# Seven PSUM banks from one pool, two queues of matmuls in product steps, and a block sum copied by VectorE, in a two-attention kernel on one core

## Chip, core and metric

The kernel runs on one core of a Trainium2 chip. The metric is the device time of one execution in microseconds. Before the change it is 1604.68 us, the median of three runs (1604.38 to 1604.77). Engine names are short: PE is TensorE's matmuls and PEld its weight loads, DVE is VectorE, ACT ScalarE, POOL GpSimd, SP SyncE.

## What is computed

Two attentions over 2048 positions, width 576, 32 heads of 18, all in float32. Their outputs stand beside each other in the result.

```python
# A: each position sees 8 positions, 2 apart (W=8, dil=2)
logits = einsum("bhsd,bhswd->bhsw", q, kg) * scale
o = einsum("bhsw,bhswd->bhsd", softmax(where(mask, logits, -1e9)), vg)
a = o.transpose(0, 2, 1, 3).reshape(B, S, D) @ wo
# B: full attention
p = softmax(einsum("bhqd,bhkd->bhqk", q, k) * scale)
o = einsum("bhqk,bhkd->bhqd", p, v)
b = o.transpose(0, 2, 1, 3).reshape(B, S, D) @ wo
return concatenate([a, b], axis=-1)
```

## The kernel before

The work has three stages. In the first (to about 430 us of the span) the inputs are multiplied by the weights; matmuls are written as sums of products of split float32 parts. `stream` deals them to the two halves of the array: rows 0 to 63 and rows 64 to 127 of TensorE each run a matmul of their own at the same time, and "half" below always means that (r = 0 is the lower, r = 1 the upper). Some of B's **maxima** are already made there; `EARLY_PAIRS` (L41) sets how many.

A maximum (`maximum`, `block`, L165 to L241) is a 128x512 block of queries by keys on TensorE (L175) and a VectorE reduce over it (L191, L193 or L205); B's softmax needs the largest logit of each query before its exponents. There are 2048 in all. A **split maximum** (`first_part`, L272) is one of them as two matmuls of 256 columns, one in each half, into one bank, with one reduce (L205).

The main stage is the loop at L1229 over steps 1 to 511. A step belongs to a block of 512 queries of four heads (32 blocks of 16 steps) and takes 128 keys: four **scores** (L305, two in each half), each followed by an exponent on ScalarE (L309), three or so maxima, and then `weigh` (L769): four matmuls of the step before's exponents by the values, each in a quarter of the array's columns, into the one bank `po`. After the 16th weigh of a block `finish` (L777) copies `po` to SBUF (L782 on VectorE where the step has a product, L784 on ScalarE elsewhere); the next block's first weigh waits for that copy, since it writes the same bank.

A step without a product (a **plain step**) writes its instructions in the order `PLAIN = "D1A30E2B"` (L50): digits are the scores (0 and 2 lower half, 1 and 3 upper), A and B a maximum in the lower and the upper half, D and E the two parts of a split one.

Steps in `TURNS` also take a piece of an output projection: of A (`sums_of_a`, L1003), or of B (`sum_of`, L1115). That is 13 or 14 matmuls of 288 columns in each half (L1107), which `beside` (L1093) writes in turn, one for one half and one for the other, with one maximum put into either half's list. After it VectorE or ScalarE takes the two banks out (L1011, L1012). Such a **product step** has its scores and other maxima before and behind the product, by `positions` (L1217). There are 34 of them with maxima, among steps 112 to 488. From step 489 on no maxima are left: the rest is scores, weighs and B's projection (the **last stage**, from about 1495 us).

PSUM has eight banks: `po` and seven others. `bank` (L90) gives these by rings (L87): scores and one half of a product go round banks 0 to 3, maxima and the other half round 4 to 6.

Of the kernel before, what the change touches and what calls it, by code (L numbers as in the profile page):

```python
# [17 lines left out]
D = 576  # L18
# [4 lines left out]
NG = H // 4  # L23
# [16 lines left out]
EARLY = 2  # L40
EARLY_PAIRS = EARLY * NB * PIECES + 2  # L41
AHEAD = 7

AT = 0

FIRST = 0

MORE = (439, 441, 451, 467, 475, 477, 484, 486)

PLAIN = "D1A30E2B"  # L50

# [18 lines left out]
def two_attentions(ctx: ExitStack, tc, xa, wa, woa, xb, wb, wob, out):  # L70
# [32 lines left out]
    do = dram.tile([2, NG - 1, 128, S], F32, name="do")  # L103
    dm = dram.tile([NG, NB, 2, 32, 128], F32, name="dm")

    po = p_po.tile([128, 512], F32, name="po")
# [58 lines left out]
    def block(g, b):  # L165
# [18 lines left out]
        def whole(r):  # L184
            k, t, p = rest[r].pop(0)
            ps = bank()
            take(ps, r, k, t, p, 0, 512)

            def reduce():
                if k < 2:  # L190
                    nc.vector.tensor_reduce(mx[:, r, p, t, k : k + 1], ps, axis=AX.X, op=ALU.max)  # L191
                else:
                    nc.vector.tensor_reduce(mx[:, r, p, t, 2 * k - 2 : 2 * k], ps.rearrange("q (h n) -> q h n", h=2),  # L193
                                            axis=AX.X, op=ALU.max)
                made(1 + (k > 1))

            return reduce

        def part(i, k, t, p, r, ps, before=None):
            if before:  # L200
                behind_of(nc.tensor.nop(nofuse=True), before)
            ins = take(ps[:, 256 * r : 256 * r + 256], r, k, t, p, 256 * i, 256)

            def reduce():
                nc.vector.tensor_reduce(mx[:, :, p, t, 2 * k - 2 + i], ps.rearrange("q (h n) -> q h n", h=2),  # L205
                                        axis=AX.X, op=ALU.max)
                made(2)

            return ins, reduce
# [62 lines left out]
    def first_part(r):  # L272

        for i in range(2):
            given[i] += 0.5
        if open_parts:
            part, args = open_parts.pop()
        else:
            rest, _, part = blocks[find(lambda rest: rest[0] and rest[1] and rest[0][-1][0] > 1)]
            piece = rest[0].pop()  # L280
            assert rest[1].pop() == piece
            args = (0, *piece)
            open_parts.append((part, (1, *piece)))
        ps = bank()
        taken = rings[ring][-1]
        ins, _ = part(*args, r, ps)

        def second():
            rings["else"].remove(taken)
            rings["else"].append(taken)  # L290
            return part(*args, 1 - r, ps, ins)[1]

        return second

# [3 lines left out]
    def score(g, b, kt, h, kind="scores"):  # L298
# [5 lines left out]
        at = slice(64 * r, 64 * r + 56)  # L304
        nc.tensor.matmul(ps, ks[at, p, 128 * kt : 128 * kt + 128], qs[at, b, p], start=True, stop=True)  # L305
        counted[0] += 1
        early = counted[0] % 8 < 6
# [103 lines left out]
    with (tc.tile_pool(name="x", bufs=1, side="right") as xp,  # L411
# [351 lines left out]
        step = 0  # L763
        projecting = False


    work = ctx.enter_context(tc.tile_pool(name="work", bufs=1, reuse_waits="tile"))
    ring = "else"
    def weigh(*steps):  # L769
        for g, b, kt, es in steps:  # L770
            for i in range(4):
                nc.tensor.matmul(po[32 * i : 32 * i + 19], vs[g][:, kt, 19 * i : 19 * i + 19], es[i],  # L772
                                 start=kt == 0, stop=kt == NT - 1)
        if kt == NT - 1:
            finish(g, b)

    def finish(g, b):  # L777
        o = work.tile([128, 512], F32, name="o", bufs=2)
        if g == NG - 1 and b == NB - 1:
            return closing(b, o, work.tile([128, 512], F32, name="rec", bufs=1))  # L780
        if step in producing:
            nc.vector.tensor_copy(o, po)  # L782
        else:
            nc.scalar.activation(o, po, AF.Copy)  # L784
        den = work.tile([128, 16], F32, name="den", bufs=2)
# [103 lines left out]
    def local(j):  # L889
# [113 lines left out]
        def sums_of_a(h):  # L1003
# [3 lines left out]
            if h == 0:  # L1007
                st["y"] = ys["a", j, st["n"]] = work.tile([128, D], F32, name="y", bufs=4)
            one, two = beside("scores", *(halves(r, 0, w, st["x"], cols, slice(0, 128), True) for r in range(2)))
            y = st["y"][:, cols]  # L1010
            nc.scalar.activation(y, two, AF.Copy)  # L1011
            behind_scores.append(lambda: nc.vector.tensor_add(y, one, y))  # L1012

# [78 lines left out]

    def beside(kind, *both):  # L1093

        sums_ = [bank(k)[:, :288] for k in (kind, None)]
        turns = [[(sums_[r], *ab, i == 0, i == len(t) - 1) for i, ab in enumerate(t)] for r, t in enumerate(both)]
        pair = kind and int(sum(given)) + 2 <= NG * NB * PIECES * 2
        if pair:

            for r in range(2):  # L1100
                turns[r].insert(6 + 4 * r, None)
        for i in range(max(map(len, turns))):
            for r in range(2):
                if i < len(turns[r]):
                    if turns[r][i]:
                        ps, a, b, start, stop = turns[r][i]
                        nc.tensor.matmul(ps, a, b, start=start, stop=stop)  # L1107
                    else:
                        maximum(r)()
        if pair:  # L1110

            rings["else"].append(rings["else"].pop(0))
        return sums_

    def sum_of(y, t, h, chunks, kind=None):  # L1115
# [9 lines left out]
        one, two = beside(kind, *both)  # L1125
        nc.vector.tensor_copy(y, one)
        nc.vector.tensor_add(y, two, y)

    def first(t, b, h):
        sums[t, b, h] = bank()[:, :288]  # L1130
        for c in range(4):
            some(sums[t, b, h], t, h, c, *olds[b][c], c == 0, False)

    def half_end(t, b, h, new):
# [4 lines left out]
        if isinstance(part, tuple):  # L1139
            ps = bank("scores")[:, :288]  # L1140
            some(ps, t, h, 4, *new, True, True)
            nc.vector.tensor_add(y, ps, part[0])
        else:
            some(part, t, h, 4, *new, False, True)
            if h == 0:
                nc.scalar.activation(y, part, AF.Copy)
            else:
                nc.vector.tensor_copy(y, part)

# [5 lines left out]
    def full(b, new):  # L1155
        def half(t, h):
            if total - int(sum(given)) > 4:
                inside.append(lambda: quarter(t, h, "scores"))
            else:
                waiting.append(lambda: quarter(t, h))  # L1160

        def quarter(t, h, *kind):
            if h == 0:
                ys[t, b] = work.tile([128, D], F32, name="y", bufs=4)
            sum_of(ys[t, b][:, 288 * h : 288 * h + 288], t, h, [*olds[b], new], *kind)
            if h == 1:
                later(1, lambda: load(out[512 * b + 128 * t : 512 * b + 128 * t + 128, D:], ys[t, b]))

        return [(4 + 2 * t + h, lambda t=t, h=h: half(t, h)) for t in range(4) for h in range(2)]

    def partial(t, h):
# [5 lines left out]
        y = ap(ys["part", t], (1, DH * SUB))[:, 288 * h : 288 * h + 288]  # L1177
        waiting.append(lambda: sum_of(y, t, h, olds[b]))
        sums[t, b, h] = (y,)
# [36 lines left out]

    def positions(n):  # L1217

        if n == 3:
            ahead = given[1] > given[0]  # L1220
            return (0, 1, 3) if ahead else (0, 1, 2)
        if n == 1:
            return (0,) if given[0] > given[1] else (1,)
        return range(4) if n > 3 else (0, 1) if n == 2 else ()

    paired = False
    due()
    step += 1
    while step < ALL:  # L1229
        n, kt = divmod(step, NT)  # L1230
        g, b = divmod(n, NB)
        many = min(4 if behind() > 0 else 3, total - int(sum(given)))
        if not inside and many in (1, 3):
            order = PLAIN if many > 1 else PLAIN.replace("A", "").replace("B", "")
        else:
            places = positions(many)
            order = "".join("%d%s" % (h, "BA"[h % 2] if h in places else "") for h in range(4))
            if inside:
                at = order.index("3" if 3 in places else "2") if step % NT != AT or AT == 0 else FIRST
                order = order[:at] + "+" + order[at:]  # L1240
        es = [None] * 4
        for c in order:
            if c in "0123":
                es[int(c)] = score(g, b, kt, int(c))
            elif c in "AB":
                maximum("AB".index(c))()
            elif c in "DE":
                if parted:
                    parted.pop()()()
                else:  # L1250
                    parted.append(first_part("DE".index(c)))
            else:
                inside.pop(0)()
        for fs in (behind_scores, outside):
# [42 lines left out]
```

## Time and profile before

| | us |
|---|---|
| time, median of three runs | 1604.68 |
| the profiled execution's own time | 1604.72 |
| its span in the profile | 1602.9 |
| TensorE matmuls busy | 1595.1 |
| VectorE busy | 1400.5 |
| ScalarE busy | 1203.0 |
| GpSimd busy | 961.6 |

The clock of TensorE was granted in full (0.999). A matmul's row covers its time in the pipeline, so rows of matmuls overlap and a busy PE need not be a PE at its peak; what a step takes is read from the start of one step's first matmul to that of the next.

### The profile page before, as it was taken

To read this page: it belongs to the slowest core of one execution; us is meant where nothing else is said; L and a number is where in the kernel's file an instruction comes from. 1 tells how busy PE (TensorE), PEld (TensorE's weight loads), DVE (VectorE), ACT (ScalarE), POOL (GpSimd) and SP (SyncE) were. 2 spreads that over 40 slices of the span, in tenths; PEclk is the share of its full clock that TensorE was granted. 3 is DMA by queue.
4 is the path that set the end of the run, shared out by engine and by line. 5 is a ranking of instruction groups with operands and counts; after the bars stand their busy time and mean duration, and the time that the engine had idled before them with its cause. 6 is when DMAs were issued, how large, how long until landed. Compare 5 with 4: busy or idle time off the path is not lost.

```text
span 1602.9 us, 34949 instructions
## 1 busy us (share of the span) xinstructions
PE 1595.1 (100%) x13360; PEld 944.4 (59%) x13360; DVE 1400.5 (87%) x2372; ACT 1203.0 (75%) x2399; POOL 961.6 (60%) x816
## 2 busy tenths in 40 slices
PE   9999999999999999999999999999999999999998
PEld 7999998888544444444444444444444444444776
DVE  5299999999999999999999999999999999999533
ACT  6423441121699999999999999999999999988544
POOL 2405742210256987985995994995995996940100
PEclk9999999999999999999999999999999999999999
DMA  8938954532321352254236235323623232234211
GB/s 248 237 125 208 272 172 122 145 106 74 68 56 54 75 117 73 68 126 112 59 78 154 63 84 139 93 58 95 128 71 94 62 84 78 61 124 152 87 39 60
DMA packets 190150, 173.13 MB, mean 108 GB/s; under 512 B 123120, under 2 KB 136944, under 8 KB 188256
## 3 DMA queue, kind: packets, MB, share of 16 engines
q1 hardware_dynamic: 185120, 159.36, 36.0%
q0 software_dynamic: 4032, 10.63, 3.2%
q8 instruction: 106, 1.74, 0.5%
q10 hardware_dynamic: 832, 0.92, 0.2%
q14 instruction: 60, 0.49, 0.1%
HBM read 97.47 MB, written 72.95 MB: 106 GB/s over the span
## 4 chain that ended last, share of the span: by engine, by line
PE 98%; DVE 1%; ACT 0%; DMA 0%; issue 0%; POOL 0%; ACTq 0%; POOLq 0%; DVEq 0%
PE po L772 31%; PE bank L305 19%; PE bank L175 19%; PE bank L394 17%; PE bank L1107 8%; PE bank L331 5%; PE bank L546 0%; DVE mx L191 0%; DMA out<-y 0%; DVE mx L193 0%; PE bank L1082 0%; ACT vs L612 0%; DVE rec L846 0%; POOL xlo L442 0%; DVE wlo L442 0%
## 5 line engine op out<-in xcount | busy, mean ns | idle before, releaser
L309 ACT ACTIVATE e<-bank 128x512 f32<-128x512 f32 x2048 | 1048.8, 606 | 72.2 <-PE bank L305 68.8
L175 PE MATMUL bank<-ks,qs 54*128 54x512 f32 (+1 forms) x2502 | 783.1, 381 | 1.0 <-DVE mx L191 0.5
L191 DVE TENSOR_REDUCE mx<-bank 128x1 f32<-128x512 f32 x1024 | 682.1, 684 | 72.7 <-PE bank L175 52.5
L175 PEld LDWEIGHTS bank<-ks,qs 54*128 54x128 f32 x2502 | 397.8, 184 | 433.9 <-DVE mx L205 334.1
L305 PE MATMUL bank<-qs,ks 56*128 56x512 f32 x2048 | 571.7, 425 | 0.0
L772 PE MATMUL po<-e,v 128*19 128x512 f32 x4096 | 537.4, 599 | 0.0
L193 DVE TENSOR_REDUCE mx<-bank 128x2 f32<-128x512 f32 x570 | 373.0, 684 | 27.7 <-PE bank L175 16.2
L305 PEld LDWEIGHTS bank<-qs,ks 56*128 56x128 f32 x2048 | 301.5, 184 | 39.9 <-ACT e L309 34.2
L205 DVE TENSOR_REDUCE mx<-bank 128x2 f32<-128x512 f32 x454 | 309.6, 682 | 0.0
L965 POOL TENSOR_TENSOR pr<-lg,akv 128x1024 f32<-128x1024 f32 x72 | 157.3, 2209 | 0.6
L772 PEld LDWEIGHTS po<-e,v 128*19 128x19 f32 x4096 | 70.6, 97 | 132.2 <-issue 123.6
L722 ACT ACTIVATE ohi<-bank 128x512 f32<-128x512 f32 (+1 forms) x56 | 30.4, 595 | 156.6 <-issue 109.4
L394 PE MATMUL bank<-xhi,ahi 64*128 64x512 f32 (+1 forms) x448 | 117.5, 390 | 0.0
L394 PE MATMUL bank<-xhi,alo 64*128 64x512 f32 (+1 forms) x448 | 111.3, 390 | 0.0
L394 PE MATMUL bank<-xlo,ahi 64*128 64x512 f32 (+1 forms) x448 | 106.5, 391 | 0.1
L917 POOL TENSOR_TENSOR pr<-aq,akv 128x1024 f32<-128x1024 f32 x40 | 87.8, 2203 | 10.4 <-PE po L772 9.3
L967 POOL TENSOR_TENSOR pr<-pr 128x512 f32<-128x512 f32 x72 | 91.5, 1296 | 0.6
L534 POOL TENSOR_TENSOR olo<-olo,ohi 128x512 fp32r<-128x512 f32 x36 | 46.1, 1293 | 67.8 <-ACT ohi L533 57.5
L442 POOL TENSOR_TENSOR alo<-raw,ahi 128x512 fp32r<-128x512 f32 (+1 forms) x14 | 17.6, 1258 | 110.9 <-ACT ahi L441 60.9
L920 POOL TENSOR_TENSOR pr<-pr,aohi 128x1024 f32<-128x1024 f32 x32 | 76.6, 2393 | 0.6
L920 POOL TENSOR_TENSOR pr<-pr 128x1024 f32<-128x1024 f32 x32 | 76.5, 2390 | 0.0
L112 POOL CAST mt<-mt 128x32 fp32r<-128x32 f32 x32 | 6.9, 217 | 113.2 <-DVE mt L222 113.2
(201 smaller groups left out, 2088.8 us busy)
## 6 DMA issues: line engine op xcount, KB each, us to landing
do<-n SPq DMA_DIRECT2D x28, 512.0 KB
da<-ohi SPq DMA_DIRECT2D x52, 256.0 KB
akv<-da SPq DMA_DIRECT2D x64, 175.5 KB
out<-y SPq DMA_DIRECT2D x32, 288.0 KB
qs<-dqk SPq DMA_DIRECT2D x30, 288.0 KB
ks<-dqk SPq DMA_DIRECT2D x30, 288.0 KB
at<-dao SPq DMA_DIRECT2D x64, 128.0 KB
rec<-drec SPq DMA_DIRECT2D x29, 256.0 KB
```

What stands on the lines that cost most here:

```text
L175: return nc.tensor.matmul(ps, qs[rows_, b, p, 128 * t : 128 * t + 128], ks[rows_, p, 512 * k + at : 512 * k + at + n], start=True, stop=True)
L191: nc.vector.tensor_reduce(mx[:, r, p, t, k : k + 1], ps, axis=AX.X, op=ALU.max)
L193: nc.vector.tensor_reduce(mx[:, r, p, t, 2 * k - 2 : 2 * k], ps.rearrange("q (h n) -> q h n", h=2), axis=AX.X, op=ALU.max)
L205: nc.vector.tensor_reduce(mx[:, :, p, t, 2 * k - 2 + i], ps.rearrange("q (h n) -> q h n", h=2), axis=AX.X, op=ALU.max)
L305: nc.tensor.matmul(ps, ks[at, p, 128 * kt : 128 * kt + 128], qs[at, b, p], start=True, stop=True)
L309: nc.scalar.activation(e, ps, AF.Exp, scale=SCALE)
L394: nc.tensor.matmul(ps, a, b, start=start, stop=stop)
L772: nc.tensor.matmul(po[32 * i : 32 * i + 19], vs[g][:, kt, 19 * i : 19 * i + 19], es[i], start=kt == 0, stop=kt == NT - 1)
L920: nc.gpsimd.tensor_add(st["prs"][0], st["prs"][0], st["prs"][c - 1])
L965: nc.gpsimd.tensor_mul(at, ap(st["lg"], (0, 2), (SUB, W), (1, SUB)), window(st["v"], n))
L967: nc.gpsimd.tensor_add(at[:, :, :4], at[:, :, :4], at[:, :, 4:])
L1107: nc.tensor.matmul(ps, a, b, start=start, stop=stop)
```

## The change

Seven edits. (1) In the main stage any of the seven banks may go to any use: `bank` takes the one that by a count came free first. The count (`busy`, `freed`, `filled`, `emptied`) adds fixed durations per instruction and half or engine; it runs when the program is written, not on the chip. (2) `PLAIN` becomes `D1A30EB2`: the upper half's maximum is written ahead of the lower half's last score. (3) In product steps every half has a queue of its own, and `in_turn` takes the next instruction from the half that the count finds less busy. (4) Their three maxima are one split maximum and one in each half. (5) `finish` always copies `po` on VectorE. (6) In the second step of a block whose first step had no product, two maxima are made instead of three. (7) `EARLY_PAIRS` rises by 6: 12 more maxima in the first stage, 12 fewer in the main stage.

```diff
-EARLY_PAIRS = EARLY * NB * PIECES + 2
+EARLY_PAIRS = EARLY * NB * PIECES + 8
...
-PLAIN = "D1A30E2B"
+PLAIN = "D1A30EB2"
...
+    busy = {0: 0, 1: 0, "ACT": 0, "DVE": 0}
+    freed = [0] * 7
+    held = {}
+
     def bank(kind=None):
+        if not projecting:
+            n = min((i for i in range(7) if i not in held), key=lambda i: freed[i])
+            held[n] = p_bank.tile([128, 512], F32, name=f"bank{n}")
+            return held[n]
...
+    def filled(r, ns, t=None):
+        n = held_as(t)
+        busy[r] = max(busy[r], 0 if n is None else freed[n] + 165) + ns
+
+    def emptied(engine, ns, r, t):
+        busy[engine] = max(busy[engine], busy[r] + 214) + ns
+        n = held_as(t)
+        if n is not None:
+            del held[n]
+            freed[n] = busy[engine] + 100
...
+        filled(r, 226, ps)
+        emptied("ACT", 490, r, ps)
...
-        if step in producing:
-            nc.vector.tensor_copy(o, po)
-        else:
-            nc.scalar.activation(o, po, AF.Copy)
+        nc.vector.tensor_copy(o, po)
+        emptied("DVE", 598, 0, None)
...
-        many = min(4 if behind() > 0 else 3, total - int(sum(given)))
+        many = min(4 if behind() > 0 else 2 if kt == 1 and step > 1 and step - 1 not in producing else 3, total - int(sum(given)))
...
+    def in_turn(queues):
+        while any(queues):
+            r = int(not queues[0] or bool(queues[1]) and busy[1] < busy[0])
+            queues[r].pop(0)()
...
+        if many == 3 or many == 1 and open_parts:
+            rows_ = ("D0A+2", "1BE+3") if many == 3 else ("D0+2", "1E+3")
+        else:
+            a, b_ = (many, 0) if many == 1 and given[0] < given[1] else (many // 2, many - many // 2)
+            rows_ = ("0" + "A" * a + "+2" if a < 2 else "0A+2A", "1" + "B" * b_ + "+3" if b_ < 2 else "B1+B3")
...
+        if many == 3 and not any(products):
+            do_all(ops[c] for c in PLAIN)
+        else:
+            in_turn([[f for c in rows_[r] for f in (products[r] if c == "+" else [ops[c]])] for r in range(2)])
```

Of the steps, 444 are plain ones with three maxima after the change (453 before), 9 are plain with two (none before), and 32 of the 34 product steps have five maxima both before and after.

On TensorE, in the product of step 144: `bank0` is the lower half's bank and `bank4` the upper's before the change, `bank1` and `bank4` after it; the 128x512 row is the maximum in the lower half. Before:

```order
L1107 MATMUL bank0_11031<-wolo_7076,at0_10733 128x288
L1107 MATMUL bank4_11032<-wolo_7076,at0_10733 128x288
L175 MATMUL bank6_11045<-ks0_89,qs0_88 128x512
L1107 MATMUL bank4_11032<-wohi_7226,at0_10733 128x288
L1107 MATMUL bank0_11031<-wohi_7226,at0_10733 128x288
L1107 MATMUL bank4_11032<-wohi_7226,at1_10737 128x288
L1107 MATMUL bank0_11031<-wohi_7226,at1_10737 128x288
L1107 MATMUL bank4_11032<-wolo_7227,at0_10733 128x288
```

And now:

```order
L1133 MATMUL bank1_11046<-wolo_7107,at0_10743 128x288
L1133 MATMUL bank4_11048<-wolo_7107,at0_10743 128x288
L197 MATMUL bank3_11060<-ks0_89,qs0_88 128x512
L1133 MATMUL bank4_11048<-wohi_7252,at0_10743 128x288
L1133 MATMUL bank4_11048<-wohi_7252,at1_10747 128x288
L1133 MATMUL bank1_11046<-wohi_7252,at0_10743 128x288
L1133 MATMUL bank4_11048<-wolo_7253,at0_10743 128x288
L1133 MATMUL bank1_11046<-wohi_7252,at1_10747 128x288
```

Behind the maximum the upper half now has two products written before the lower half's next one; before it was one and one.

On ScalarE, at the end of block 4 (steps 80 and 81; exponents and the copy of the block sum), before:

```order
L309 ACTIVATE e<-bank_8733 128x512 [waits PE_49]
L309 ACTIVATE e<-bank_8740 128x512 [waits PE_49]
L784 ACTIVATE o<-po 128x512 [waits DMAHW0_49,PE_49,Pool_49]
L309 ACTIVATE e<-bank_8760 128x512 [waits PE_49]
L309 ACTIVATE e<-bank_8767 128x512 [waits PE_49]
```

And now that copy on VectorE, between the reduces of steps 80 (three above it), 81 (two) and 82:

```order
L216 TENSOR_REDUCE mx<-bank_8742 128x2
L230 TENSOR_REDUCE mx<-bank_8736 128x2
L216 TENSOR_REDUCE mx<-bank_8756 128x2
L806 COPY o<-po 128x512
L216 TENSOR_REDUCE mx<-bank_8782 128x2
L216 TENSOR_REDUCE mx<-bank_8785 128x2
L214 TENSOR_REDUCE mx<-bank_8810 128x1
```

The copy leaves ScalarE's row of exponents and takes the place of one reduce on VectorE.

On ScalarE, the exponents of plain steps 163 and 164, with what each waits for (`Activation_49` is ScalarE's own count of finished work, which says that a tile of exponents may be written again). Before:

```order
L309 ACTIVATE e<-bank_11755 128x512 [waits PE_49]
L309 ACTIVATE e<-bank_11762 128x512 [waits PE_49]
L309 ACTIVATE e<-bank_11766 128x512 [waits PE_49]
L309 ACTIVATE e<-bank_11773 128x512 [waits PE_49]
L309 ACTIVATE e<-bank_11789 128x512 [waits PE_49]
```

And now:

```order
L330 ACTIVATE e<-bank_11764 128x512 [waits PE_49,Activation_49]
L330 ACTIVATE e<-bank_11771 128x512 [waits PE_49,Activation_49]
L330 ACTIVATE e<-bank_11775 128x512 [waits PE_49]
L330 ACTIVATE e<-bank_11785 128x512 [waits PE_49]
L330 ACTIVATE e<-bank_11798 128x512 [waits PE_49,Activation_49]
```

A second wait is a separate instruction ahead of the exponent. There are 88 such rows before and 808 after: scores whose bank VectorE emptied no longer tell ScalarE that its own older work is done.

More of the change, by code (lines that the diff above doesn't have):

```diff
@@ L194, in reduce @@
                                             axis=AX.X, op=ALU.max)
+                emptied("DVE", 598, r, ps)
                 made(1 + (k > 1))
@@ L206, in reduce @@
                                         axis=AX.X, op=ALU.max)
+                emptied("DVE", 598, r, ps)
                 made(2)
@@ L284, in first_part @@
         ps = bank()
-        taken = rings[ring][-1]
         ins, _ = part(*args, r, ps)
[L288 to L293, printed above, removed]
+        return lambda: part(*args, 1 - r, ps, ins)[1]
     e_room = None
@@ L764, in two_attentions @@
         projecting = False
+        busy.update({0: 0, 1: 0, "ACT": 0, "DVE": 0})
+        for i, n in enumerate(rings["scores"] + rings["else"]):
+            freed[n] = i
     work = ctx.enter_context(tc.tile_pool(name="work", bufs=1, reuse_waits="tile"))
@@ L1091, in two_attentions, with beside, one, alone @@
     waiting = []
[L1093 to L1115, printed above, removed]
+    def beside(*both):
+        sums_ = [None, None]
+        def one(r, i, a, b):
+            if i == 0:
+                sums_[r] = bank()
+            nc.tensor.matmul(sums_[r][:, :288], a, b, start=i == 0, stop=i == len(both[r]) - 1)
+            filled(r, 133, None if i else sums_[r])
+        return [[lambda r=r, i=i, ab=ab: one(r, i, *ab) for i, ab in enumerate(t)] for r, t in enumerate(both)], sums_
+    def in_turn(queues):
+        while any(queues):
+            r = int(not queues[0] or bool(queues[1]) and busy[1] < busy[0])
+            queues[r].pop(0)()
+    def alone(queues, end):
+        for fs in zip(*queues):
+            do_all(fs)
+        end()
+    def sum_of(y, t, h, chunks):
         pos, cols = slice(128 * t, 128 * t + 128), slice(288 * h, 288 * h + 288)
```

98 lines of the change are left out of this document (51 added, 47 removed).

## The prediction

> **What bounds the kernel now.** I read the page first, then busy time by stage, then single steps in order of time.
>
> ```profile
> PE 1595.1 (100%) x13360; PEld 944.4 (59%) x13360; DVE 1400.5 (87%) x2372; ACT 1203.0 (75%) x2399; POOL 961.6 (60%) x816
> ...
> PE 98%; DVE 1%; ACT 0%; DMA 0%; issue 0%; POOL 0%; ACTq 0%; POOLq 0%; DVEq 0%
> ```
>
> The chain that ended last is TensorE for 98% of the span, so only what shortens or lengthens TensorE's row of steps counts. Its rows overlap in the pipeline, so "100%" doesn't say that it is at its peak. By stage (us, then busy time and instructions of each engine):
>
> ```profile
> 120.00:400.00 280.00, 279.89 (x2419) 258.47 (x2417) 269.91 (x446) 81.15 (x153) 100.22 (x113) 1.00 0.56 157
> 440.00:1490.00 1050.00, 1049.78 (x8541) 478.51 (x8538) 987.81 (x1678) 992.72 (x1959) 820.13 (x649) 1.00 0.35 91
> 1495.00:1595.00 100.00, 99.59 (x1136) 72.72 (x1133) 33.50 (x78) 48.63 (x95) 3.36 (x8) 1.00 0.13 46
> ```
>
> In the main stage VectorE and ScalarE are busy 94% and 95% of the time, so three engines run close together and a lost 0.1 us of one may reach the others. A plain step there, TensorE alone:
>
> ```profile
> 908.89 0.38 PE L175 MATMUL bank<-ks,qs 54*128 54x256 f32 x1
> 908.89 0.49 PE L305 MATMUL bank<-qs,ks 56*128 56x512 f32 x1
> 909.11 0.39 PE L175 MATMUL bank<-ks,qs 54*128 54x512 f32 x1
> ...
> 909.46 0.31 PE L175 MATMUL bank<-ks,qs 54*128 54x256 f32 x1
> ...
> 909.62 0.39 PE L175 MATMUL bank<-ks,qs 54*128 54x512 f32 x1
> 909.94 1.05 PE L772 MATMUL po<-e,v 128*19 128x512 f32 x8
> 910.92 0.38 PE L175 MATMUL bank<-ks,qs 54*128 54x256 f32 x1
> ```
>
> The step starts at 908.89 and the next at 910.92: **2.03 us**, of which 1.05 are scores and maxima and 0.98 the weigh.
>
> **The change part by part.** The sum is made against the profiled execution's own 1604.72 us (its span of 1602.9 and 1.8 around it), which is 0.04 over the median of the runs.
>
> *Product steps, 32 with equal work before and after.* Two kinds alternate in the order before. Where the lower half is ahead in maxima, the upper gets the third one, and the other way round. Step 192 has 2 scores, 3 maxima and 14 products in the lower half, and 2, 2 and 13 in the upper:
>
> ```profile
> 824.23 0.50 PE L305 MATMUL bank<-qs,ks 56*128 56x512 f32 x1
> ...
> 825.36 0.50 PE L1107 MATMUL bank<-wohi,at 64*128 64x288 f32 x4
> 825.63 0.37 PE L1107 MATMUL bank<-wolo,at 64*128 64x288 f32 x2
> ...
> 825.83 0.40 PE L175 MATMUL bank<-ks,qs 54*128 54x512 f32 x1
> ...
> 826.07 0.43 PE L1107 MATMUL bank<-wohi,at 64*128 64x288 f32 x3
> ...
> 827.46 1.05 PE L772 MATMUL po<-e,v 128*19 128x512 f32 x8
> ...
> 828.44 0.38 PE L175 MATMUL bank<-ks,qs 54*128 54x256 f32 x1
> ```
>
> It takes 828.44 - 824.23 = 4.21 us. Four products start within 825.63 - 825.36 = 0.27, so a pair, one in each half, takes 0.135. A matmul of 512 columns holds its half for 826.07 - 825.83 = 0.24. The lower half is the long one: 5 x 0.24 + 14 x 0.135 = 3.09, against 4 x 0.24 + 13 x 0.135 = 2.72. Now step 144, with 2, 2 and 14 below and 2, 3 and 13 above, so 2.85 and 2.96:
>
> ```profile
> 719.06 0.49 PE L305 MATMUL bank<-qs,ks 56*128 56x512 f32 x1
> ...
> 721.77 0.60 PE L305 MATMUL bank<-qs,ks 56*128 56x512 f32 x2
> ...
> 722.30 1.05 PE L772 MATMUL po<-e,v 128*19 128x512 f32 x8
> ...
> 723.28 0.38 PE L175 MATMUL bank<-ks,qs 54*128 54x256 f32 x1
> ```
>
> It takes 4.22, though its longer half is 0.13 shorter than step 192's. So writing the two halves in strict turn costs about 0.14 here: while one half works off its inserted maximum, the other one gets a single product. After the change every such step has 4 matmuls of 512, one of 256 and 14 products in the lower half, and one product less in the upper. The order listing shows two upper products behind a lower maximum, so strict turns are gone. Step 192 loses half of 0.24, and I take 4.10 for both kinds: 0.11 and 0.12 less, over 16 + 16 steps **-3.7 us**. The one pair of rows in which a 256-column matmul is followed in its half (909.46 to 909.62) has 0.16 instead of 0.12, which would leave 0.07 and 0.08 a step, -2.4; if the strict turns cost nothing it is less still, which is the first rival.
>
> *The end of a block without a product, 9 times* (steps 80 to 82):
>
> ```profile
> 584.56 1.51 DVE L193 TENSOR_REDUCE mx<-bank 128x2 f32<-128x512 f32 x2
> ...
> 584.73 0.38 PE L175 MATMUL bank<-ks,qs 54*128 54x256 f32 x1
> ...
> 585.16 0.63 ACT L784 ACTIVATE o<-po 128x512 f32<-128x512 f32 x1
> ...
> 585.84 0.14 PEld L772 LDWEIGHTS po<-e,v 128*19 128x19 f32 x8 [0.30 <-ACT o L784]
> ...
> 586.83 0.18 PEld L175 LDWEIGHTS bank<-ks,qs 54*128 54x128 f32 x1 [0.85 <-DVE mx L205]
> ...
> 587.80 0.18 PEld L305 LDWEIGHTS bank<-qs,ks 56*128 56x128 f32 x1 [0.23 <-ACT e L309]
> ...
> 588.23 0.14 PEld L772 LDWEIGHTS po<-e,v 128*19 128x19 f32 x8 [0.24 <-issue]
> ...
> 589.22 0.18 PEld L175 LDWEIGHTS bank<-ks,qs 54*128 54x128 f32 x1 [0.85 <-DVE mx L205]
> ```
>
> The copy on ScalarE puts four exponents back, and the next step's scores wait for their banks (0.23 at 587.80): the two steps take 2.10 and 2.39. On VectorE, where product steps have it already, it lasts this long (mean ns behind the busy time):
>
> ```profile
> L782 DVE COPY o<-po 128x512 f32<-128x512 f32 x21 | 14.5, 691 | 2.7 <-PE po L772 2.1 <-POOL ao L971 0.2
> ```
>
> It comes behind the reduce that starts at 584.56; the two reduces take 1.51, so one about 0.7, and the copy runs from about 585.2 to 585.9. The weigh behind it starts 0.06 later than now, 2.16 for the first step. Two maxima instead of three in that step pay for the copy on VectorE (0.69 each), and the wait for `po` covers what TensorE would gain by them. Late next are the reduces, which need no more time than in a plain step, so the second step takes 2.03: 4.19 instead of 4.49, 9 x 0.30 = **-2.7 us**. If the reduces stay behind it is half of that.
>
> *Twelve maxima moved.* In the first stage 2419 matmuls take 280 us, 0.116 each: **+1.4 us**. VectorE is at 269.91 of 280 there; 12 reduces in the rest of that stage are hidden. If they were not, they would cost up to 12 x 0.7 = 8. In the main stage 9 of the 12 are those just counted, and 3 go from the last product step that has any: 2 of 512 columns in its longer half, **-0.5 us**.
>
> *Plain steps, 444.* `PLAIN` keeps the sequence within each half, and seven banks serve eight matmuls a step as before. Two small things change, and they pull opposite ways. The maximum no longer stands behind a score that may wait for ScalarE: the gap 909.46 to 909.62 would shrink from 0.16 to 0.12, and at most half of the 0.04 is lasting, since ScalarE sets the pace of that bank; 444 x 0.02 gives -8.9. On the other side 720 exponents get a second wait as an instruction of its own. Those there are now, and four exponents in a row:
>
> ```profile
> L309 ACTq EVENT_SEMAPHORE  x34: 17/17/17, 654.3 to 1395.0; - x34
> ```
>
> ```profile
> 1503.52 2.06 ACT L309 ACTIVATE e<-bank 128x512 f32<-128x512 f32 x4 [4.08 <-PE bank L305]
> ```
>
> 720 x 17 ns is 12.2 us if every one lengthened its step, and nothing if the slack takes them: 2.06 includes the tail of the last, which the next one overlaps. I take 0 for both together, and keep -8.9 and +12.2 as the ends.
>
> *The last stage.* This is the wait that seven free banks might remove (us, times, longest):
>
> ```profile
> PEld bank L1107 <- DVE y L1126: 3.2, 11, 0.3
> ```
>
> The order still has these products in the bank that VectorE is just emptying, since scores and two sums need eight: 0, at best -3.2.
>
> Sum: 1604.72 - 3.7 - 2.7 + 1.4 - 0.5 = **1599.2 us**, 0.34% faster.
>
> **The rivals.** *The halves are independent.* Then a product step takes its longer half: 16 steps lose 0.11, and the other 16 go from 2.96 to 4 x 0.24 + 0.12 + 14 x 0.135 = 2.97, no gain. The term becomes -1.8 and the time 1601.1. The two steps above speak against it, the shorter load took longer. The Trainium skill has the rule: TensorEngine Tiling (Array Packing), section Tiling Modes, says under Key Properties that tiles work independently and load weights and multiply in parallel. By that rule, 1601.1; the rows of step 144 don't agree.
>
> *The count is off.* Fixed durations leave out the small reduces and transposes of VectorE, so a product's first matmul finds its bank still being emptied, as it does now in some steps. 0.1 us in 33 steps brings 3.3 back: 1602.5. The change would then not do what its count says.
>
> *ScalarE's waits end up on the path, slower.* In a plain step ScalarE's four exponents, the banks that they free and the next scores make a ring that is nearly full (95% busy). With two waits of 17 ns in most steps it would pace TensorE: 1599.2 + 12.2 = 1611.4. It decides from (1604.7 - 1599.2) / 444 = 12 ns a step on.
>
> *The maximum ahead of the score pays.* 1599.2 - 8.9 = 1590.3, if ScalarE's ring has room.
>
> **How the numbers follow.** Forecast 0.48; independent halves 0.15; count off 0.12; ScalarE slower 0.12; plain steps faster 0.13. 0.2% is 3.2 us, about what a measurement of this kernel can tell from no change. Faster by more (under 1601.5) are the forecast nearly whole, the plain steps, and half of the independent halves: 0.66. Within it: 0.20. Slower: 0.14, the ScalarE case and reduces late in the first stage. The range goes from 1592.5, most of the way to 1590.3, to 1606.5, which leaves out the worse half of the ScalarE case.
>
> **What would show it.** Product steps of 4.10 from first matmul to next step's, in both kinds; end-of-block steps of 2.16 and 2.03; plain steps still 2.03 with 17 ns waits between exponents; last stage of equal length; the first stage 1.4 longer. Plain steps of 2.05 or more, or 2.01 or less, would prove the sum wrong, since there are 444 of them.

## The result, and the profile after

The changed kernel takes **1610.06 us**, the median of six runs (1609.37 to 1611.65), against 1604.58 for the kernel before in the same comparison (1604.32 to 1604.77). The ratio is 1.0035, 95% interval 1.0023 to 1.0047: slower by a third of a per cent, where 0.34% faster was forecast. Times of kernels are medians of executions at full clock (0.999 to 1.000); one of the ten of the kernel with the block-end part undone ran at 0.752, took 1855.61 us and is left out.

The busy times hardly moved, and TensorE is still nearly all of the chain (98% before), so the page alone doesn't say why. The changed kernel's page, busy time by engine and the chain that ended last:

```profile
PE 1598.1 (99%) x13384; PEld 937.1 (58%) x13384; DVE 1401.1 (87%) x2381; ACT 1204.8 (75%) x2390; POOL 961.1 (60%) x816
...
PE 95%; DVE 2%; DMA 2%; issue 1%; POOL 1%; ACT 0%; SPq 0%; POOLq 0%; ACTq 0%; DVEq 0%
```

By stage it is plainer (us, then busy time and instructions of each engine), the same three stretches as before:

```profile
120.00:400.00 280.00, 279.90 (x2417) 243.53 (x2415) 275.04 (x454) 80.58 (x152) 100.06 (x113) 1.00 0.54 156
440.00:1490.00 1050.00, 1048.96 (x8510) 483.46 (x8509) 980.06 (x1672) 992.83 (x1948) 820.25 (x645) 1.00 0.35 90
1495.00:1595.00 100.00, 100.00 (x1157) 73.31 (x1157) 33.40 (x74) 50.68 (x98) 3.50 (x8) 1.00 0.15 53
```

In the 1050 us of the main stage TensorE starts 8510 matmuls, 8541 before, though the whole program now has 24 more (13384 and 13360): the loss is there, while the clock is full in both. Single steps show its form. TensorE in three steps that follow each other (the row of 256 columns opens a step, the row x8 is its weigh):

```profile
1001.19 0.38 PE L197 MATMUL bank<-ks,qs 54*128 54x256 f32 x1
...
1002.25 1.05 PE L796 MATMUL po<-e,v 128*19 128x512 f32 x8
1003.23 0.38 PE L197 MATMUL bank<-ks,qs 54*128 54x256 f32 x1
...
1004.33 1.05 PE L796 MATMUL po<-e,v 128*19 128x512 f32 x8
1005.32 0.38 PE L197 MATMUL bank<-ks,qs 54*128 54x256 f32 x1
...
1007.36 0.38 PE L197 MATMUL bank<-ks,qs 54*128 54x256 f32 x1
```

The steps last 2.04, 2.09 and 2.04. In the long one the weigh begins 1.10 behind the opening, in the one ahead of it 1.06; before, the median step was like the short one (2.036). Two plain steps together take 4.127 us in the median, 4.073 before (403 pairs each): 0.05 us in every second step, some 10 us in all.

What stands ahead of it is on ScalarE. The second waits, all of one length, and the first exponent of the steps that opened at 1001.19 and 1005.32:

```profile
L330 ACTq EVENT_SEMAPHORE  x808: 17/17/17, 415.8 to 1592.8; - x162
```

```profile
1001.78 0.60 ACT L330 ACTIVATE e<-bank 128x512 f32<-128x512 f32 x1
```

```profile
1005.91 0.60 ACT L330 ACTIVATE e<-bank 128x512 f32<-128x512 f32 x1
```

They start 0.59 us after the opening. Before, in the step that opened at 908.89, it was 0.53:

```profile
909.42 0.60 ACT L309 ACTIVATE e<-bank 128x512 f32<-128x512 f32 x1
```

Over all steps: TensorE's signal that the first score is done comes 22 to 23 ns ahead of the exponent where there is no second wait (the kernel before), and 82 to 83 ns where there is one (the changed kernel); over 450 exponents in each, and 9 in 10 lie within 2 ns of that. The signal itself comes 0.51 us behind the step's opening in both. So the wait costs **60 ns at the first exponent of a step**, not the 17 of its row. The other three exponents start some 0.48 to 0.49 us behind each other with a second wait or without: there it is hidden.

Two other places stand as forecast. Step 192 opens at 827.13 and the next at 831.24, 4.11 us:

```profile
827.13 0.38 PE L197 MATMUL bank<-ks,qs 54*128 54x256 f32 x1
...
830.25 1.05 PE L796 MATMUL po<-e,v 128*19 128x512 f32 x8
831.24 0.38 PE L197 MATMUL bank<-ks,qs 54*128 54x256 f32 x1
```

And at the end of block 4 VectorE's row takes the copy (L806) between its reduces, ScalarE's is free of it, and the weigh waits for it a little longer than before (0.41, on TensorE's weight loads):

```profile
586.46 0.68 DVE L216 TENSOR_REDUCE mx<-bank 128x2 f32<-128x512 f32 x1
587.06 0.68 DVE L806 COPY o<-po 128x512 f32<-128x512 f32 x1
587.65 1.28 DVE L216 TENSOR_REDUCE mx<-bank 128x2 f32<-128x512 f32 x2
```

```profile
587.79 0.14 PEld L796 LDWEIGHTS po<-e,v 128*19 128x19 f32 x8 [0.41 <-DVE o L806]
```

### The profile page after: what moved, and what is told of

It reads as the page before. It is cut to its first block, busy times and chain, and to the rows that moved or that the text cites. A ratio compares the mean times of both kernels' runs of the same rounds, so it can differ in the third digit from the quotient of the medians.

```text
span 1608.1 us, 35753 instructions
## 1 busy us (share of the span) xinstructions
PE 1598.1 (99%) x13384; PEld 937.1 (58%) x13384; DVE 1401.1 (87%) x2381; ACT 1204.8 (75%) x2390; POOL 961.1 (60%) x816
## 4 chain that ended last, share of the span: by engine, by line
PE 95%; DVE 2%; DMA 2%; issue 1%; POOL 1%; ACT 0%; SPq 0%; POOLq 0%; ACTq 0%; DVEq 0%
PE po L796 31%; PE bank L197 18%; PE bank L324 17%; PE bank L415 16%; PE bank L1133 8%; PE bank L352 5%; DMA drec<-den 1%; DVE mx L214 1%; POOL xlo L463 0%; DMA akv<-da 0%; DVE mx L230 0%; DVE o L806 0%; PE bank L567 0%; DMA dqk<-ohi 0%; DMA out<-y 0%
## 5 line engine op out<-in xcount | busy, mean ns | idle before, releaser
L197 PE MATMUL bank<-ks,qs 54*128 54x256 f32 (+1 forms) x2526 | 763.5, 377 | 1.5 <-ACT ohi L743 0.9
L197 PEld LDWEIGHTS bank<-ks,qs 54*128 54x128 f32 x2526 | 395.1, 185 | 459.7 <-ACT e L330 371.1
L324 PEld LDWEIGHTS bank<-qs,ks 56*128 56x128 f32 x2048 | 296.6, 184 | 15.2 <-ACT e L330 9.3
L940 POOL TENSOR_TENSOR aohi<-aq,akv 128x1024 f32<-128x1024 f32 x32 | 70.5, 2204 | 0.9
```

What stands on the lines that cost most here:

```text
L197: return nc.tensor.matmul(ps, qs[rows_, b, p, 128 * t : 128 * t + 128], ks[rows_, p, 512 * k + at : 512 * k + at + n], start=True, stop=True)
L940: nc.gpsimd.tensor_mul(pr, ap(st["q"][:, 2 * c], (SUB, 2), (0, W), (1, SUB)), window(st["k"], c))
```

## The experiments

**Theory A** came from these rows. A second wait delays the first exponent of a step, because ScalarE has nothing running ahead of it. The delay goes round a ring: a step's last exponent frees the bank of the next step's last score, behind which stands that step's weigh, behind it the first score of the step after, and its first exponent. The ring is two steps long, so 60 ns make about 30 a step. The waits come from the one pool: where a score takes a bank that VectorE emptied last, TensorE's signal no longer implies that ScalarE's own old work is done.

**Rivals:** B, the count gives banks that the chip frees later; C, the new order `D1A30EB2` costs; A2, every second wait costs, wherever it stands.

Every time below has the kernel before beside it, at 1604.6 to 1604.7 us. "Plain" is the mean of the plain steps with three maxima (444, or 453 where marked +), "product" that of 32 product steps, "first waits" how many of some 475 first exponents carry a second wait.

| kernel | us | ratio, 95% | plain | product | first waits |
|---|---|---|---|---|---|
| before | 1604.58 | | 2.053+ | 4.266 | 1 |
| changed | 1610.06 | 1.0023 to 1.0047 | 2.068 | 4.152 | 449 |
| new order alone | 1604.66 | 0.9990 to 1.0008 | 2.052+ | 4.264 | 1 |
| banks by last emptier, all steps | 1607.01 | 1.0007 to 1.0026 | 2.046 | 4.311 | 4 |
| same, first score only | 1629.28 | 1.0141 to 1.0172 | 2.099 | 4.302 | 21 |
| same, all but the first score | 1616.22 | 1.0056 to 1.0090 | 2.068 | 4.322 | 443 |
| same, plain steps only | **1600.81** | 0.9966 to 0.9986 | 2.048 | 4.134 | 44 |
| that, wait on second exponents | 1601.62 | 0.9973 to 0.9991 | 2.050 | 4.130 | 44 |
| that, wait on first exponents | 1611.11 | 1.0027 to 1.0054 | 2.070 | 4.139 | 445 |
| that, block-end part undone | 1600.48 | 0.9966 to 0.9983 | 2.053+ | 4.142 | 36 |
| changed, strict turns | 1611.44 | 1.0027 to 1.0057 | 2.071 | 4.138 | 449 |
| changed, old product row | 1611.99 | 1.0031 to 1.0064 | 2.068 | 4.196 | 424 |
| changed, divided pool | 1658.17 | 1.0318 to 1.0349 | 2.051 | 5.370 | 2 |
| that, strict turns | 1641.33 | 1.0212 to 1.0246 | 2.047 | 4.949 | 2 |

### The new order alone

```diff
-PLAIN = "D1A30E2B"
+PLAIN = "D1A30EB2"
```

> The kernel before, with only the order of the plain step changed: half E ahead of maximum B. Its rings of banks stay, so 85 second waits as before. Theory A: the swap itself is free or a small gain, up to 17 ns per plain step, so 1597 to 1605 us. Theory C (the swap costs): 10 us more, 1612 to 1616.

1604.66 us and a ratio of 0.9999: no gain and no loss. C falls, and with it the gain of 8.9 us that the prediction kept as an end.

### Banks by the engine that emptied them last

```diff
+    by = ["ACT"] * 4 + ["DVE"] * 3
...
-            n = min((i for i in range(7) if i not in held), key=lambda i: freed[i])
+            now = min(busy[0], busy[1])
+            n = min((i for i in range(7) if i not in held),
+                    key=lambda i: (max(freed[i], now), (by[i] == "ACT") != (kind == "scores"), freed[i]))
...
             del held[n]
+            by[n] = engine
```

> The changed kernel, with one addition to the count: among the PSUM banks that the count holds free by now, a score takes one that ScalarE emptied last, and every other product one that VectorE emptied last. Of the 2048 exponents 81 then carry a second wait, for ScalarE's own older work (85 in the kernel before, 805 in the changed one). Theory A (a second wait ahead of the first exponent of a step starts that exponent some 61 ns later, and the ring of exponents, scores and banks passes about 30 ns of it to every plain step): the mean plain step falls from 2.068 us to 2.02 to 2.04, and the time to 1596 to 1601 us. Theory B (the count gives banks later or earlier than the chip frees them, and TensorE waits for a bank): the count stays, so the time stays at 1607 to 1612. Theory C (the order of the plain step, with the half E ahead of the maximum B, is what costs): also 1607 to 1612.

The time, 1607.01, misses A's range. By stage A holds: the plain steps fall from 2.068 to 2.046, 9.5 us in all, while the product steps rise from 4.152 to 4.311, 5.1 us. In a product step the preference moves other matmuls too, and up to four of one half's products now stand on end instead of three.

### Only the first score prefers, and all but the first

```diff
-                    key=lambda i: (max(freed[i], now), (by[i] == "ACT") != (kind == "scores"), freed[i]))
+                    key=lambda i: (max(freed[i], now), (by[i] == "ACT") != (kind in ("scores", "s1")), freed[i]))
...
-        ps = bank(kind)
+        ps = bank(f"s{h}" if kind == "scores" and not projecting else kind)
```

(For the other kernel `"s0", "s2", "s3"` in place of `"s1"`.)

> As the kernel whose scores prefer banks emptied by ScalarE, but only the first score of a step (number 1) prefers them; the other three prefer banks emptied by VectorE. In the steady steps 324 of some 475 third exponents of a step carry a second wait, and 21 first ones, 32 second ones and 10 fourth ones. Theory A (only the first exponent of a step has nothing running ahead of it that hides the wait): within 3 us of the kernel in which all four prefer, so 1596 to 1602 us. Rival A2 (each second wait costs ScalarE some time wherever it stands): 324 steps times 30 ns is 10 us more than that kernel, so 1606 to 1612.

> The reverse of the kernel before it: scores 0, 2 and 3 of a step prefer banks that ScalarE emptied last, score 1 one that VectorE emptied. In the steady steps 443 of some 475 first exponents carry a second wait, and 21 of all the others together. Theory A: as slow as the changed kernel, 1607 to 1613 us, although it has 300 second waits fewer than it. Rival A2 (every second wait costs alike): 460 waits of 805, so a little over half of the loss, about 1604 to 1606. Theories B and C: 1607 to 1612 too, so they part from A only by the other two kernels.

With all but the first, the plain steps take 2.068, as in the changed kernel, with 276 second waits fewer (529 and 805): for A, against A2. The time is above A's range by what the product steps lose (4.322, 5.5 us in 32). With only the first, A predicted no loss and the kernel lost 25 us: an experiment with two changes in it. In 283 plain steps the third score now gets the bank of the step before's last maximum, which VectorE empties late. What its scores' weight loads waited for:

```profile
  DVE mx L218: 35.1, 178
  DVE mx L220: 12.5, 60
  DVE mx L234: 7.9, 10
```

B's mechanism exists, then, but it isn't in the changed kernel: there these loads wait 15.2 us in all, 9.3 of them for ScalarE. On A2 this kernel tells nothing.

### The preference in plain steps alone, and two kernels that move one wait

These fix what each matmul of a plain step should get, v for a bank that VectorE emptied and s for one that ScalarE did; other steps go by the count as in the changed kernel.

```diff
+            now = min(busy[0], busy[1])
+            want = wants and wants.pop(0)
+            n = min((i for i in range(7) if i not in held),
+                    key=lambda i: (max(freed[i], now), by[i] != want, freed[i]) if want else freed[i])
...
         if many == 3 and not any(products):
+            wants += [{"v": "DVE", "s": "ACT"}[c] for c in "vsvssvs"]
```

`"vssvsvs"` gives the second waits to second exponents, `"vvsssvs"` to first ones. Both exchange the bank of the maximum in the middle with that of one score.

> The changed kernel, and only in its plain steps does a score take a bank that ScalarE emptied last and every other product one that VectorE emptied last; in all other steps the count gives the bank that is free first, as in the changed kernel. 149 second waits on ScalarE's exponents (805 in the changed kernel), 44 of them on a first exponent of a step. The kernel that prefers so in every step measured 908.5 us for the 444 plain steps (918.0 in the changed kernel, so 9.5 us less) and 137.9 us for the 32 product steps (132.9, so 5.1 us more). Theory A (the wait ahead of a step's first exponent): the first is kept and the second is gone, so 1610.1 less 9.5, about 1600.5 us (1599 to 1603). If the product steps need the preference of the plain steps around them to be absent too, their 5.1 us come back: about 1605.

> As the kernel with the preference in plain steps only, but the second score of a plain step takes a bank that VectorE emptied and the maximum ahead of it one that ScalarE emptied: 223 second exponents of a step carry a second wait more, no other. Theory A (only in front of a step's first exponent has ScalarE nothing running that hides the wait): within 2 us of the kernel with the preference in plain steps. Rival A2 (each second wait costs some 21 to 30 ns wherever it stands): 5 to 7 us more than it.

> As the kernel with the preference in plain steps only, but the first score of a plain step takes a bank that VectorE emptied and the maximum behind it one that ScalarE emptied: 445 first exponents of a step carry a second wait in place of 44. Theory A: the loss of the changed kernel's plain steps comes back, 8 to 12 us more than the kernel with the preference, about 1609 to 1613. Theory B (banks late, not waits): no loss, since both banks are free by the count in either case.

All three come as A has it. Without the waits 1600.81; with 223 on second exponents 0.8 us more, where A2 wanted 5 to 7 (its median plain step is 2.035 in both; 0.7 of the 0.8 stands in one step, 82, which takes 3.72 against 3.02); with 445 on first exponents 10.3 more. Two plain steps together take 4.070, 4.070 and 4.127 us. With the wait (220 plain steps) and without it (224), a second exponent starts 0.494 us behind the first: there the wait costs nothing. B is out for this pair too: with the waits on first exponents and without them, TensorE's signal for the first score comes 0.51 us behind the step's opening. The three kernels' second waits, all of one length:

```profile
L336 ACTq EVENT_SEMAPHORE  x152: 17/17/17, 415.8 to 1583.6; - x152
```

```profile
L336 ACTq EVENT_SEMAPHORE  x373: 17/17/17, 415.9 to 1584.7; - x187
```

```profile
L336 ACTq EVENT_SEMAPHORE  x587: 17/17/17, 416.7 to 1594.6; - x196
```

An opening of a plain step and its first exponent, without the waits (0.54 between them, also the median) and then with them on first exponents (0.63; the median is 0.60):

```profile
1002.62 0.38 PE L203 MATMUL bank<-ks,qs 54*128 54x256 f32 x1
```

```profile
1003.16 0.60 ACT L336 ACTIVATE e<-bank 128x512 f32<-128x512 f32 x1
```

```profile
1002.72 0.38 PE L203 MATMUL bank<-ks,qs 54*128 54x256 f32 x1
```

```profile
1003.35 0.60 ACT L336 ACTIVATE e<-bank 128x512 f32<-128x512 f32 x1
```

The main stage without the waits has 8613 matmuls where the changed kernel has 8510:

```profile
440.00:1490.00 1050.00, 1048.36 (x8613) 479.87 (x8612) 986.12 (x1684) 991.46 (x1954) 824.39 (x651) 1.00 0.35 91
```

A row that looks like proof is none. In the changed kernel's page 371.1 us of idle time of the maxima's weight loads are put down to ScalarE, and 315.1 here to VectorE. Both rows hold the time of every weigh (0.85 a step), and their sums agree:

```profile
L197 PEld LDWEIGHTS bank<-ks,qs 54*128 54x128 f32 x2526 | 395.1, 185 | 459.7 <-ACT e L330 371.1
```

```profile
L203 PEld LDWEIGHTS bank<-ks,qs 54*128 54x128 f32 x2526 | 394.6, 184 | 460.0 <-DVE mx L236 315.1
```

### The end of a block undone

From the kernel with the preference in plain steps:

```diff
-EARLY_PAIRS = EARLY * NB * PIECES + 8
+EARLY_PAIRS = EARLY * NB * PIECES + 2
...
-        nc.vector.tensor_copy(o, po)
-        emptied("DVE", 598, 0, None)
+        if step in producing:
+            nc.vector.tensor_copy(o, po)
+            emptied("DVE", 598, 0, None)
+        else:
+            nc.scalar.activation(o, po, AF.Copy)
+            emptied("ACT", 490, 0, None)
...
-        many = min(4 if behind() > 0 else 2 if kt == 1 and step > 1 and step - 1 not in producing else 3, total - int(sum(given)))
+        many = min(4 if behind() > 0 else 3, total - int(sum(given)))
```

> As the kernel with the preference in plain steps only (1600.8 us), with the end-of-block part undone: block sums copied by ScalarE outside the product steps, three maxima and not two in those steps, and 12 maxima fewer in the first stage. By the terms: first stage 1.3 us less, the nine steps at a block's end and the nine behind them 3.2 us more, 1.9 us more in all, so 1602 to 1603.5. Rival (with ScalarE no longer behind, its copy is hidden and the first stage's maxima are pure loss): 1.3 us less, 1599 to 1600.

1600.48: no difference that can be told, and between the two ranges. In the traces the nine pairs of steps rise from 38.6 to 40.3 us, and step 2 opens 0.7 us earlier (422.8 and 422.1), so the part is worth 1.0. As much again is lost in one step, 82, which takes 3.02 in the kernel with the part, where the other eight of its kind take 2.03 (without the part all nine take 2.38 to 2.39): one of its maxima waits for the keys that it reads. That this comes from the maxima made earlier is likely, but not shown by a run of its own. TensorE there, in the kernel with the part:

```profile
PE bank L203 <- DMA ks<-dqk: 0.7, 1, 0.7
```

### Product steps: turns, row, pool

Strict turns put back, in the changed kernel:

```diff
-            r = int(not queues[0] or bool(queues[1]) and busy[1] < busy[0])
-            queues[r].pop(0)()
+            for r in range(2):
+                if queues[r]:
+                    queues[r].pop(0)()
```

The old row of scores, whole maxima and products:

```diff
+            if any(products):
+                order = "0B1A2+3A" if given[1] > given[0] else "0B1A+2B3"
+                for c in order:
+                    do_all([f for fs in zip(*products) for f in fs] if c == "+" else [ops[c]])
...
```

The divided pool:

```diff
-            n = min((i for i in range(7) if i not in held), key=lambda i: freed[i])
+            mine = [i for i in rings["scores" if kind == "scores" else "else"] if i not in held]
+            n = min(mine or [i for i in range(7) if i not in held], key=lambda i: freed[i])
...
-                sums_[r] = bank()
+                sums_[r] = bank("else" if r else "scores")
```

> The changed kernel with only the order within its product steps put back: the queues of the two halves are emptied strictly in turn, in place of whichever half has less engine time counted. Theory: turns are what the product steps gained by, so their mean goes from 4.15 us back to 4.23 to 4.27, and the time rises by 2.5 to 3.7 us, to about 1613. Rival (the gain is from the seven banks given out by the count, which stay): no change, 1609 to 1611.

> The changed kernel with the row of a product step as before: one row for both halves, three whole maxima in their old places among the scores, the products in strict turn at the old place; the banks still come from the one pool by the count. Theory P: product steps stay near 4.13 to 4.16 us, so the time stays at 1609 to 1611. Rival (the order, with two half maxima in place of one whole, is the gain): they go back to 4.23 to 4.27, 2.5 to 3.7 us more: 1612.5 to 1614.

> The changed kernel with its pool divided again: scores, and the products' sums of the lower half, take one of banks 0 to 3, all else one of banks 4 to 6, and within a part the count gives the bank that is free first. 73 second waits on ScalarE's exponents, 2 of them on a first exponent. Strict turns in the product steps left their mean at 4.14 us, so turns are not what they gained by. Theory P (the one pool of seven is): plain steps at 2.045 to 2.055 us in the mean, so 9 us less than in the changed kernel, and product steps at 4.27 to 4.32, 4 to 5 us more: 1604 to 1606 us. Rival (the pool gains nothing; the order of scores, maxima and products in the product step does): product steps stay at 4.13 to 4.16, and the time is 1600 to 1602.

> The divided pool again, with strict turns in the product steps, since the count with a divided pool had written six products of one half on end (two at most before the change, three in the changed kernel) and made the product steps 5.37 us long. What is left to compare: new row of scores and maxima with one pool and strict turns 4.14 us, old row with one pool and strict turns 4.20, old row with divided pool and strict turns (the kernel before) 4.27; this one is the new row with divided pool and strict turns. Theory P (the one pool is worth 0.07 us a step whatever the row): 4.20 to 4.23, plain steps 2.046 to 2.052, time 1601.5 to 1604. Theory R (the row alone is worth it): 4.13 to 4.16, time 1599.5 to 1602. If it were the banks together with the row, 4.27 or more, 1604 or more.

Strict turns leave the product steps at 4.138 (4.152 in the changed kernel): the queue by the count is worth nothing. (Of the 1.4 us that this kernel takes more, 0.7 stand in step 82, 3.12 against 2.41, and as much in the other plain steps.) The old row in the one pool takes 4.196, so the pool is worth 0.070 us a step under the old row, and the new row 0.058 more under strict turns. The mean hides that each works in one kind of step alone. The kinds are those of the order before, 16 steps each, mean:

| kernel | as step 144 | as step 192 |
|---|---|---|
| before: old row, divided banks, strict turns | 4.309 | 4.223 |
| old row, one pool, strict turns | 4.166 | 4.226 |
| new row, one pool, strict turns | 4.154 | 4.123 |
| changed: new row, one pool, turns by the count | 4.165 | 4.138 |

The pool takes 0.14 from step 144's kind (0.10 by the median, since a few steps before were later still) and nothing from the other; the new row takes 0.10 from step 192's kind and 0.01 from step 144's. Other edits part the first two kernels too, but outside of the product steps; of these, the new order of the plain steps alone left the product steps at 4.264. The new row under a divided pool takes 4.949, outside of both theories' ranges and in the third that was written beside them: row and pool go together. Its three maxima ahead of the product use all three banks of their part, so the upper half's sum takes one that this very step's maximum has just filled, and TensorE waits for VectorE; the lower half's sum often waits for ScalarE. What the products' weight loads (PEld) waited for in that kernel:

```profile
PEld bank L1134 <- DVE mx L215: 12.6, 21, 0.8
PEld bank L1134 <- ACT e L331: 9.5, 23, 0.9
```

The first divided pool was confounded: the count answered it by writing six products of one half on end. That made its steps 0.42 longer than strict turns do; in step 192 the wait for the bank ends at the same place in both, 1.52 us behind the opening. The times of these two kernels also hold a last stage of some 120.5 us, 106.8 in the changed kernel; why was not looked into.

## Why the prediction was wrong

**Plain steps: the step that failed.** "I take 0 for both together, and keep -8.9 and +12.2 as the ends" was out by 10 us. The gain from the maximum ahead of the score, taken from a gap of 0.04 us, is not there (new order alone, 0.9999). The loss is: 444 steps at 22 ns, 9.8 us, from the pair of kernels with and without the waits on first exponents. From the kernel before to the changed one it is the same: the 435 plain steps of three maxima that both have, those behind a block's end left aside, went from 889.4 to 899.3 us. Two readings led astray. The price was the 17 ns of the wait's own row, but the exponent behind it starts 60 ns later; and "nothing if the slack takes them" rested on a row of four exponents on end, where it is true, while the first exponent of a step stands alone. The rival with ScalarE's waits on the path had the mechanism, its place and 1611.4; it got 0.12. Its sum of 720 waits at 17 ns came so near by luck: the runs show some 450 that count, at 60 ns, shared out over a ring of two steps. Its threshold of 12 ns a step was right, and 22 is above it.

**The end of a block** was right: the nine pairs went from 40.44 to 37.67 us, -2.8 for -2.7. **The first stage** rose by 1.3 for 1.4. **The last stage** stayed equal on TensorE (100.9 us). **The last product steps** gave 0.3 for 0.5. A term of 0.6 was not in the sum: what comes behind the last matmul, which ends in the DMA of the result, is that much longer in the changed kernel's profile. With the product steps these make up the 5.2 us between the two spans (1602.9 and 1608.1).

**Product steps** fell by 3.66 us for 3.7, but for other reasons than forecast, so half of that number was luck. "writing the two halves in strict turn costs about 0.14 here" falls with the strict-turns kernel: what step 144 lost beyond its longer half was the divided banks, and the 0.14 went with the one pool while the turns stayed strict. The new row gave step 192's kind 0.10, where halving a maximum was to give 0.11. The rival of independent halves had this right for both kinds, 0.11 and nothing; its 1601.1 didn't come either, since it left out what the pool gives step 144's kind, and the waits of the plain steps. The rule of the Trainium skill (TensorEngine Tiling (Array Packing), section Tiling Modes, Key Properties), that tiles work independently, fits strict turns (4.138 and 4.152 us) better than my reading did. Independence has a limit here: six products of one half on end cost 0.42 us.

**"The count is off"** didn't happen in the changed kernel, and does as soon as a bank goes to a use that the count prices wrongly (first score only).

Without the first exponents' waits the sum comes out: 1600.81 measured, 1599.2 forecast. Most of what is left is the wait for keys in step 82 (1.0). That kernel beats both, by 0.24% and 0.57%. Not shown is what the 43 ns beside the wait's own 17 consist of; no row covers them. The ring itself was read from order and waits, and its length from the pairs of steps; no kernel broke it.

## What to carry to other kernels

A pool that gives out whichever buffer is free changes more than lateness: a buffer that another engine emptied brings a second wait for the instruction that takes it over, so let a use prefer buffers that its own reader emptied, where that moves nothing else (in the product steps here it cost 5.1 us). Price such a wait by where it stands: nothing in a queue that runs back to back, several times its own row ahead of an instruction that starts on a fresh signal, and then ask whether that engine is in a ring with the bound one. Judge an edit by the mean of each kind of step, and where work is split between two halves, by which half is the long one; a time of two terms of opposite sign shows neither.

## Not expected of the hardware

A second wait whose condition has long been met costs 60 ns of start on ScalarE at an exponent that was waiting (from 22 or 23 to 82 or 83 ns behind TensorE's signal), and nothing at a second exponent, 0.494 us behind the first with it and without. Two halves of the array written in strict turn lose nothing against a balanced order (4.138 and 4.152 us), yet six matmuls on end for one half lose 0.42 us a step (5.370 and 4.949, with divided banks).
